# A hybrid attention and gated-MLP kernel on one core: the first four tiles are centred instead of normalised, and the value weights come in two halves

## The chip, the core and the metric

The kernel runs on one core of a Trainium2 chip. The metric is device time in microseconds (us). Three runs of the kernel before took 222.53, 222.60 and 222.67 us; the median, 222.6 us, is the time before.

The engines are named as the profile names them: PE is the matrix engine (PEld its weight loads), DVE the vector engine, ACT the scalar engine, POOL the GpSimd engine, and SP the engine that issues the DMAs (SPq in the profile).

## The reference

The input x has 2048 tokens of 512 features. It is layer-normalised without gain or bias, and two branches and the input itself are added.

```
xn  = (x - mean) / sqrt(var + 1e-5)
q, k, v = xn @ wqkv                            # 32 heads of 16 features
phi_q = [softmax(q @ w_phi), softmax(-(q @ w_phi))]      # per head
phi_k = [softmax(k @ w_phi), softmax(-(k @ w_phi))]
kv, z = sum over tokens of phi_k v, and of phi_k
A   = (phi_q kv) / (phi_q z + 1e-6) @ wo
B   = ((xn @ w_gate) * (xn @ w_up)) @ w_down   # 1792 inner features
out = x + A + B
```

## The kernel before

**Tiles.** The tokens form 16 tiles of 128. The kernel works from xnT, the normalised input with features on the partitions, four blocks of 128 features wide.

**Making xnT.** For each tile DVE takes mean and variance (L410, L412), POOL makes 1/sqrt(var + 1e-5) with a power (L419, after an addition at L417, which DVE does for tiles 0 to 3), and DVE subtracts and multiplies in one instruction (L434, `emit_xn`). Tiles 0 to 3 are then transposed by PE, four 128-column matmuls against an identity, and ACT copies the result out of PSUM (`act_op`, L277). Tiles 4 to 15 are transposed by DMA (L164), which SP issues.

**Keys and values.** `k_pe(t)` makes the values of tile t on PE (four 512-column matmuls with `wv`) and ACT copies them to `vext`. `wprime` folds the small head matrices (`wbd`, built by POOL from w_phi at L392, `make_wbd`) into the transposed key or query weights `wT`. `k_pk(t)` makes the key features on PE; `emit_exp` copies them with both signs by two ACT instructions, takes maxima on DVE (L474, L480) and exponentials on ACT; `k_norm` normalises them on DVE.

**The MLP.** `glu(g, ft)` is a unit of four token tiles (group g) by 128 inner features (ft): four 512-column matmuls for the gate, four for the up projection, an ACT copy and a DVE product (L545). `final(t)` adds the down projection and the attention output and x (DVE L642), and SP stores it.

**Queries.** `q_pk`, `q_scale`, `q_T` (a DMA transpose), `q_num` (PE, then DVE L614, L615) and `q_oT` (a DMA transpose) run tile by tile once the sums over all tokens are there.

**What sets the order.** Every operation is recorded as a step by one helper for each engine, so one line of the profile (L297 for all matmuls, L277 for all ACT work) stands for many places. `_order` then plans: each step has an estimated cost and each load a due time (`at`); whenever an engine is free in the plan, it takes the earliest ready step, and among those ready the one of lowest priority number. MLP units have numbers of 1e6 and more, so they fill holes; steps marked `urgent` (the first four tiles' normalisation and transposes) are taken up to 200 ns ahead of others. The order of each engine is then fixed, and on the chip an engine waits for its next step even when a later one could run. SP's loads all go into one hardware queue, in the order of issue.

**The start.** SP issues x of tile 0, tile 1, tiles 2 and 3, the whole `wv`, x of tiles 4 to 7, the gate and up weights of the first four units (512 KB each), w_phi, the transposed key weights `wT` (a DMA transpose), then the gate and up weights of the other ten units (1280 KB each), then the transposes of tiles 4 to 7. PE first runs 46 matmuls on zeros. Then come the transposes and values of tiles 0 to 3, four MLP units, `wprime` and four `k_pk`, and then the work on tile 4.

Of the kernel before, what the change touches and what calls it, by code (L numbers as in the profile page):

```python
# [197 lines left out]
def _build(nc, es, A_x, A_wqkv, A_w_phi, A_wo, B_w_gate, B_w_up, B_w_down, out):  # L198
# [93 lines left out]
    def mms(items, prio=None, warm=False):  # L292

        def fn(e):
            ins = None
            for o, l, r, a, z in items:
                ins = e.matmul(o, lhsT=l, rhs=r, start=a, stop=z)  # L297
            return ins
        reads = []
        writes = []  # L300
        c = 0.0
        for o, l, r, a, z in items:
            reads += [l, r]
            writes.append(o)
            c += max(25.0, o.free_size() / 2.4 + 2.3) * (1.6 if warm else 1.0)
        return sc.step(PE, fn, reads=reads, writes=writes, cost=c, lat=260.0, prio=prio)
# [40 lines left out]
    def load_gu(on, f0, n, at):  # L347
# [3 lines left out]

    load_x(SP, 0, 1, 3150.0)
    load_x(SP, 1, 1, 3700.0)
    load_x(SP, 2, 2, 4800.0)
    load_w(SP, wv_v, A_wqkv[:, 1024:1536].rearrange("(q p) j -> p q j", p=128), 6800.0)
    load_x(SP, 4, 4, 8200.0)
    load_gu(SP, 0, 4, 10800.0)
    sc.dma(SP, wphi_v, bass.AP(tensor=A_w_phi.tensor, offset=A_w_phi.offset, ap=[[16, 128], [2048, NQ], [1, 16]]),
           at=12500.0)
    load_wT(1, 14500.0)  # L360
    load_gu(SP, 4, 10, 20500.0)


    zero = sbv("tree", 0, 128)
    dve(lambda e: e.memset(zero, 0.0), [], [zero], 128)  # L365
    mms([(bank(7, 0, 128), zero, zero, True, True)] * 46, warm=True)

# [37 lines left out]
    pool(lambda e: e.memset(mhalf, -0.5), [], [mhalf], 4)  # L405

    def emit_ln_stats(t0, n):
        ts = slice(t0, t0 + n)
        for t in range(t0, t0 + n):
            dve(lambda e, t=t: e.bn_stats(stats_v[:, t, 0:6], x_tile(t)), [x_tile(t)], [stats_v[:, t, 0:6]], 512)  # L410
        for t in range(t0, t0 + n):
# [3 lines left out]
        rstd4 = rstd_v[:, ts, 0:1]  # L415
        add = dve if t0 < 4 else pool
        add(lambda e: e.tensor_scalar(out=veps.unsqueeze(2), in0=var4, scalar1=1e-5, scalar2=None, op0=ALU.add),  # L417
            [mv_v[:, ts, :]], [veps], n)
        pool(lambda e: e.tensor_tensor(out=rstd4, in0=veps.unsqueeze(2), in1=mhalf[:, 0:n].unsqueeze(2), op=ALU.pow),  # L419
# [8 lines left out]
    def next_a():  # L428
        b = a_bank[0] % a_banks[0]
        a_bank[0] += 1  # L430
        return b

    def emit_xn(t):
        dve(lambda e: e.tensor_scalar(out=xn_tile(t), in0=x_tile(t), scalar1=mv_v[:, t, 0:1],  # L434
                                      scalar2=rstd_v[:, t, 0:1], op0=ALU.subtract, op1=ALU.mult),
            [x_tile(t), mv_v[:, t, 0:1], rstd_v[:, t, 0:1]], [xn_tile(t)], 512, rate=0.5)
        if t >= 4:
            sc.dma(SP, xnT_v[:, :, t * 128:(t + 1) * 128], xn_tile(t), transpose=True, issue=1250.0, land=3200.0,
                   at=36000.0 + 1300.0 * (t - 8) if t >= 8 else 22500.0 + 1300.0 * (t - 4))
            return  # L440
        b = next_a()
        mms([(bank(b, q * 128, 128), xn_tile(t)[:, q * 128:(q + 1) * 128], ident, True, True) for q in range(NQ)])
        act_op(xnT_v[:, :, t * 128:(t + 1) * 128], bank(b).rearrange("p (q s) -> p q s", q=NQ))

# [15 lines left out]

    def emit_exp(src_bank, e_out):

# [3 lines left out]
        tr = (i % 2) * 1024  # L466
        act_op(pst[:, 0:512], bank(src_bank))
        act_op(pst[:, 512:1024], bank(src_bank), scale=-1.0)
        src = pst.rearrange("p (g k) -> p g k", g=16)
# [33 lines left out]

    def k_pe(t):
        b = next_a()
        mms(group(bank(b), [(xnT(q, t * 128, 128), wv_v[:, q, :]) for q in range(NQ)]))
        act_op(vext_all[:, t, :, 0:64], bank(b).rearrange("p (c j) -> p c j", c=8))

    def k_pk(t):
        b = next_a()  # L510
        mms(group(bank(b), [(xnT(q, t * 128, 128), Wp_v[:, 1, q, :]) for q in range(NQ)]))
        p_slot["k", t] = emit_exp(b, ek_v[:, t, :])

# [73 lines left out]
    def q_pk(t):  # L587
        b = next_q()
        mms(group(bank(b), [(xnT(q, t * 128, 128), Wp_v[:, 0, q, :]) for q in range(NQ)]))
        p_slot["q", t] = emit_exp(b, eq(t))  # L590

# [17 lines left out]
    def q_num(t):  # L609
# [4 lines left out]
        dve(lambda e: e.reciprocal(out=w, in_=nd[:, :, 64:68]), [nd[:, :, 64:68]], [w], 32, rate=6.0)  # L614
        dve(lambda e: e.tensor_tensor(  # L615
            out=o.rearrange("p (g h d) -> p g h d", g=8, h=4),
            in0=nd[:, :, 0:64].rearrange("p g (h d) -> p g h d", h=4),
            in1=w[:, :, :, None].to_broadcast([128, 8, 4, 16]), op=ALU.mult),
            [nd[:, :, 0:64], w], [o], 512)

# [7 lines left out]
    def final(t, b, cols=(0, 512)):  # L628
# [12 lines left out]
        xs = x_tile(t)[:, c0:c1]  # L641
        dve(lambda e: e.tensor_tensor(out=og, in0=ob, in1=xs, op=ALU.add), [ob, xs], [og], c1 - c0, prio=-2.0)  # L642
        sc.dma(SP, out_flat[t * 128:(t + 1) * 128, c0:c1], og, is_out=True)
# [21 lines left out]

    for t in range(4):
        first = len(sc.steps)
        ln(t, 1)
        for st in sc.steps[first:]:
            st.urgent = True  # L670
        k_pe(t)
    make_wbd()
    wprime(1)
    for b0 in range(0, NT, 4):
# [5 lines left out]
        if b0 == 0:  # L680
            load_later(lambda: load_x(SP, 8, 8, 29000.0))
        if b0 == 4:
# [187 lines left out]
```

## Time and profile before

| what | value |
|---|---|
| three runs, median | 222.6 us (222.53 to 222.67) |
| the profiled execution's own time | 222.43 us |
| its span, first to last instruction | 220.7 us |
| PE busy | 215.4 us, 1273 matmuls recorded |
| DVE busy | 192.8 us |
| ACT busy, POOL busy | 114.4 us, 9.6 us |
| DMA | 19.91 MB, 8.67 MB of it read from HBM |
| granted PE clock | 1.00 throughout |

The profile is one execution. Its page gives busy time by engine, busy shares in 40 slices of 5.5 us, the DMA queue's packets, the chain of work that ended last, and groups of instructions by line with the idle time before them. The timeline view lists instructions in order of time and merges neighbours of one kind; a line's columns are start, duration (of the merged stretch), engine, line, operation, shapes, count, and in brackets the idle time before it and what ended that. The view of DMAs gives the time from issue to landing.

### The profile page before, as it was taken

The numbers are of one execution on the slowest core, as the hardware profiler recorded it, in microseconds if no ns is written. First come the engines' busy times: TensorE is split into PE (matmuls) and PEld (weight loads), VectorE is DVE, ScalarE is ACT, GpSimd is POOL, SyncE is SP. The second block draws the span as 40 slices with busy tenths as digits, with TensorE's granted clock in tenths as the row PEclk, the third lists the DMA queues.
The fourth block names the chain that finished last, engine by engine and source line by source line (L and its number), as shares of the span: only waits on it lengthen the run. The fifth ranks groups of instructions, "written<-read, shape, count | busy, mean of one in ns | idle before, by whom it ended". The sixth has DMA issues, their size and how long they took to land.

```text
span 220.7 us, 3555 instructions
## 1 busy us (share of the span) xinstructions
PE 215.4 (98%) x1273; PEld 107.0 (48%) x1296; DVE 192.8 (87%) x552; ACT 114.4 (52%) x189; POOL 9.6 (4%) x25
## 2 busy tenths in 40 slices
PE   8899999999999999999999999999999999999995
PEld 8454444444445545444445544444445454444544
DVE  5855999999998289999999999999999999998421
ACT  2668977466442699875543676656454433230000
POOL 4250000200003000000000000000000000000000
PEclk9999999999999999999999999999999999999999
DMA  6999720139200340000000004435446556565621
GB/s 175 324 295 287 177 80 3 25 74 337 88 3 19 77 95 3 0 0 0 3 0 1 3 0 87 79 74 97 95 95 98 117 107 133 77 142 118 99 72 49
DMA packets 46386, 19.91 MB, mean 90 GB/s; under 512 B 37408, under 2 KB 45344, under 8 KB 46368
## 3 DMA queue, kind: packets, MB, share of 16 engines
q1 hardware_dynamic: 46368, 19.68, 38.5%
q8 instruction: 10, 0.16, 0.3%
q14 instruction: 8, 0.07, 0.1%
HBM read 8.67 MB, written 2.10 MB: 49 GB/s over the span
## 4 chain that ended last, share of the span: by engine, by line
PE 94%; DMA 3%; SPq 1%; issue 1%; DVE 1%
PE ps L297 94%; DMA arena<-in_A_x_dram 3%; SPq L165 1%; DVE arena L410 0%; DVE arena L434 0%; DVE arena L642 0%
## 5 line engine op out<-in xcount | busy, mean ns | idle before, releaser
L297 PE MATMUL ps<-arena 128*128 128x512 bf16 (+4 forms) x1273 | 215.4, 331 | 3.0 <-DVE arena L365 1.0
L297 PEld LDWEIGHTS ps<-arena 128*128 128x128 bf16 x1296 | 107.0, 100 | 111.2 <-ACT arena L277 2.2
L277 ACT ACTIVATE arena<-ps 128x512 bf16<-128x512 f32 (+1 forms) x156 | 83.2, 596 | 53.2 <-PE ps L297 45.3
L277 ACT ACTIVATE arena<-arena 128x1024 bf16<-128x1024 bf16 x32 | 34.3, 1082 | 28.2 <-DVE arena L480 25.9
L494 DVE TENSOR_TENSOR arena<-arena 128x512 f32<-128x512 bf16 (+3 forms) x128 | 48.8, 393 | 0.1
L545 DVE TENSOR_TENSOR arena<-ps,arena 128x512 bf16<-128x512 f32 x56 | 38.0, 679 | 3.9 <-ACT arena L277 2.2
L474 DVE TENSOR_TENSOR arena<-arena 128x512 bf16<-128x512 bf16 (+3 forms) x128 | 31.6, 269 | 4.6 <-ACT arena L277 4.4
L480 DVE TENSOR_TENSOR arena<-arena 128x1024 bf16<-128x1024 bf16 x32 | 21.5, 673 | 0.0
L642 DVE TENSOR_TENSOR arena<-ps,arena 128x512 bf16<-128x512 f32 (+2 forms) x17 | 11.1, 651 | 7.4 <-PE ps L297 7.2
L410 DVE BATCH_NORM_STATS2 arena<-arena 128x6 f32<-128x512 bf16 x16 | 10.7, 681 | 1.5 <-DMA arena<-in_A_x_dram 1.5
L521 DVE TENSOR_TENSOR arena<-arena 128x1024 bf16<-128x1024 bf16 x16 | 10.9, 680 | 0.0
L615 DVE TENSOR_TENSOR arena<-ps,arena 128x512 bf16<-128x512 f32 x16 | 10.8, 673 | 0.1
L614 DVE RECIPROCAL arena<-ps 128x32 f32<-128x32 f32 x16 | 5.6, 348 | 3.7 <-PE ps L297 3.5
L518 DVE RECIPROCAL arena<-arena 128x64 bf16<-128x64 f32 x16 | 8.6, 539 | 0.0
L434 DVE TENSOR_SCALAR arena<-arena 128x512 bf16<-128x512 bf16 x16 | 6.1, 406 | 2.2 <-issue 1.5
L601 DVE TENSOR_TENSOR arena<-arena 128x512 bf16<-128x512 bf16 x16 | 6.5, 407 | 0.0
L419 POOL TENSOR_TENSOR arena<-arena 128x1 f32<-128x1 f32 (+1 forms) x7 | 5.3, 764 | 4.1 <-DVE arena L417 3.8
L598 DVE RECIPROCAL arena<-arena 128x32 f32<-128x32 f32 x16 | 5.4, 336 | 0.0
L417 POOL TENSOR_SCALAR arena<-arena 128x4 f32<-128x4 f32 x3 | 1.1, 380 | 55.1 <-DVE arena L412 55.1
L599 DVE TENSOR_TENSOR arena<-arena 128x32 bf16<-128x32 f32 x16 | 2.7, 171 | 0.0
L412 DVE BATCH_NORM_AGGREGATE arena<-arena 128x2 f32<-128x6 f32 x16 | 2.0, 160 | 0.1
L561 DVE TENSOR_TENSOR arena<-ps,arena 128x65 f32<-128x65 f32 x8 | 1.6, 220 | 0.4 <-PE ps L297 0.4
(19 smaller groups left out, 9.8 us busy)
## 6 DMA issues: line engine op xcount, KB each, us to landing
out_dram<-arena SPq DMA_DIRECT2D x15, 128.0 KB, 2.0
arena<-in_B_w_down_dram SPq DMA_DIRECT2D x1, 1792.0 KB, 7.5
arena<-in_B_w_gate_dram SPq DMA_DIRECT2D x1, 1280.0 KB, 6.8
arena<-in_B_w_up_dram SPq DMA_DIRECT2D x1, 1280.0 KB, 10.3
arena<-in_A_x_dram SPq DMA_DIRECT2D x1, 1024.0 KB, 5.4
arena<-arena SPq DMA_TRANSPOSE x44, 2.8
arena<-in_A_wqkv_dram SPq DMA_DIRECT2D x1, 512.0 KB, 4.2
arena<-in_A_x_dram SPq DMA_DIRECT2D x1, 512.0 KB, 5.7
```

The source lines that it names most:

```text
L277: return e.activation(out=out_ap, in_=in_ap, func=func, scale=scale, **kw)
L297: ins = e.matmul(o, lhsT=l, rhs=r, start=a, stop=z)
L410: dve(lambda e, t=t: e.bn_stats(stats_v[:, t, 0:6], x_tile(t)), [x_tile(t)], [stats_v[:, t, 0:6]], 512)
L474: dve(lambda e, dst=dst, src=src, k=k: e.tensor_tensor(out=dst, in0=src[:, :, 0:k], in1=src[:, :, k:2 * k], op=ALU.max), [src], [dst], 16 ...
L480: dve(lambda e: e.tensor_tensor(out=p4, in0=p4, in1=src[:, :, None, :].to_broadcast([128, 16, 16, 4]), op=ALU.subtract), [pst, src], [pst] ...
L494: dve(lambda e, dst=dst, src=src, k=k: e.tensor_tensor(out=dst, in0=src[:, :, 0:k], in1=src[:, :, k:2 * k], op=ALU.add), [src[:, :, 0:2 * ...
L518: dve(lambda e: e.reciprocal(out=rs, in_=sm), [sm], [rs], 64, rate=6.0)
L521: dve(lambda e: e.tensor_tensor(out=e4, in0=e4, in1=r4[:, :, None, :].to_broadcast([128, 16, 16, 4]), op=ALU.mult), [ek_v[:, t, :], rs], [ ...
L545: dve(lambda e: e.tensor_tensor(out=dst, in0=bank(bu), in1=gr, op=ALU.mult), [bank(bu), gr], [dst], 512, prio=-1.0)
L601: dve(lambda e: e.tensor_tensor(out=e1, in0=e1, in1=rs[:, :, None, :].to_broadcast([128, 8, 16, 4]), op=ALU.mult), [e1, rs], [e1], 512, ra ...
L615: dve(lambda e: e.tensor_tensor(out=o.rearrange("p (g h d) -> p g h d", g=8, h=4), in0=nd[:, :, 0:64].rearrange("p g (h d) -> p g h d", h= ...
L642: dve(lambda e: e.tensor_tensor(out=og, in0=ob, in1=xs, op=ALU.add), [ob, xs], [og], c1 - c0, prio=-2.0)
```

## The change

- **Centring.** Tiles 0 to 3 are centred only (`x - mean`, `emit_centred`). The factor 1/sqrt(var + 1e-5), called rstd, is still made (`emit_root`, both steps on POOL) and is put back later: as the scale of ACT's copies of the values and of the key and query features, while the MLP's product of two unscaled projections is multiplied by rstd squared in `final`, together with the attention output, which `q_num` has divided by rstd squared beforehand. One DVE reciprocal of four numbers (`emit_squares`) gives rstd squared.
- **Sign copy.** For these tiles the second copy in `emit_exp`, with the minus sign, reads the first copy in SBUF instead of PSUM.
- **Tile 1's mean** comes from ACT, as a copy of x with scale 1/512 into PSUM bank 6 and a running sum; its variance is taken by DVE after the centring.
- **Tile 0's transposes** go in two halves of two feature blocks, each with a copy of its own. Its first matmuls with `wv` are split in two steps likewise.
- **Values of tiles 0 and 1** are made in two halves of 256 columns, the second halves after the transposes of tile 2.
- **Loads.** `wv` comes in two halves of 256 columns, x of tiles 2 and 3 in a load each between them; the first gate and up weights go ahead of x of tiles 4 to 7. The due times are changed.
- **Warm-up.** 28 matmuls on zeros instead of 46, and three more after tile 0's transposes; in the plan such a matmul costs 1.92 instead of 1.6 times a fast one.

```diff
-    load_x(SP, 0, 1, 3150.0)
-    load_x(SP, 1, 1, 3700.0)
-    load_x(SP, 2, 2, 4800.0)
-    load_w(SP, wv_v, A_wqkv[:, 1024:1536]..., 6800.0)
-    load_x(SP, 4, 4, 8200.0)
-    load_gu(SP, 0, 4, 10800.0)
+    load_x(SP, 0, 1, 3000.0)
+    load_x(SP, 1, 1, 3450.0)
+    load_wv(0, 4800.0)
+    load_x(SP, 2, 1, 5200.0)
+    load_x(SP, 3, 1, 5600.0)
+    load_wv(1, 6800.0)
+    load_gu(SP, 0, 4, 9600.0)
+    load_x(SP, 4, 4, 11000.0)
     sc.dma(SP, wphi_v, ...,
-           at=12500.0)
-    load_wT(1, 14500.0)
-    load_gu(SP, 4, 10, 20500.0)
+           at=11200.0)
+    load_wT(1, 13100.0)
+    load_gu(SP, 4, 10, 19500.0)
...
-    mms([(bank(7, 0, 128), zero, zero, True, True)] * 46, warm=True)
+    mms([(bank(7, 0, 128), zero, zero, True, True)] * 28, warm=True)
...
+    def emit_centred(t):
+        mean = mv_v[:, t, 0:1]
+        if t == 1:
+            mean = lnt_v[:, 2, 8:9]
+            sc.step(ACT, lambda e: e.activation(out=bank(6), in_=x_tile(t), func=ACTF.Copy, scale=1.0 / 512.0,
+                                                accum_out=mean), ...)
+        else:
+            emit_moments(t)
+        dve(lambda e: e.tensor_scalar(out=xn_tile(t), in0=x_tile(t), scalar1=mean, scalar2=None, op0=ALU.subtract), ...)
...
+    def emit_root(t):
+        pool(lambda e: e.tensor_scalar(out=veps(t), in0=mv_v[:, t, 1:2], scalar1=1e-5, scalar2=None, op0=ALU.add), ...)
+        pool(lambda e: e.tensor_tensor(out=rstd_v[:, t, 0:1], in0=veps(t), in1=mhalf[:, 0:1], op=ALU.pow), ...)
...
+    def scale_of(t):
+        return rstd_v[:, t, 0:1] if t < RAW else 1.0
...
-                   at=36000.0 + 1300.0 * (t - 8) if t >= 8 else 22500.0 + 1300.0 * (t - 4))
+                   at=36000.0 + 1300.0 * (t - 8) if t >= 8 else 21500.0 + 600.0 * (t - 4))
...
-        act_op(pst[:, 0:512], bank(src_bank))
-        act_op(pst[:, 512:1024], bank(src_bank), scale=-1.0)
+        act_op(pst[:, 0:512], bank(src_bank), scale=scale_of(t))
+        act_op(pst[:, 512:1024], bank(src_bank) if t >= RAW else pst[:, 0:512], scale=-1.0)
...
+        if t < RAW:      # q_num
+            dve(lambda e: e.scalar_tensor_tensor(out=o4, in0=n4, scalar=veps(t), in1=w4, op0=ALU.mult, op1=ALU.mult), ...)
+            return
...
+        if t < RAW:      # final
+            r2 = lnt_v[:, 2, t:t + 1]
+            dve(lambda e: e.scalar_tensor_tensor(out=og, in0=ob, scalar=r2, in1=xs, op0=ALU.mult, op1=ALU.add), ...)
...
-    for t in range(4):
+    for t in range(RAW):
         first = len(sc.steps)
-        ln(t, 1)
+        emit_centred(t)
+        emit_T(t, 2 if t == 0 else 1)
         for st in sc.steps[first:]:
             st.urgent = True
-        k_pe(t)
+        if t == 0:
+            mms([(bank(7, 0, 128), zero, zero, True, True)] * 3, warm=True).deps.append(sc.by_eng[PE][-2])
+        if t == 1:
+            emit_moments(t)
+        emit_root(t)
+        if t < 2:
+            k_pe(t, 5 + t, 0, 256)
+        else:
+            if t == 2:
+                for s in (0, 1):
+                    k_pe(s, 7 if s == 0 else next_a(), 256, 512)
+            k_pe(t)
     make_wbd()
+    emit_squares()
     wprime(1)
```

## The prediction

> **What bounds the kernel now.** I read the page's busy times first, then the chain, then the timeline of the first 23 us, then the DMA view.
>
> ```profile
> PE 215.4 (98%) x1273; PEld 107.0 (48%) x1296; DVE 192.8 (87%) x552; ACT 114.4 (52%) x189; POOL 9.6 (4%) x25
> PE 94%; DMA 3%; SPq 1%; issue 1%; DVE 1%
> ```
>
> PE is the bound. In the chain in order of time PE starts late and then hardly stops:
>
> ```profile
> 2.70 5.72 DMA arena<-in_A_x_dram
> 8.44 0.69 DVE arena L410
> 9.14 0.33 DVE arena L434
> 9.51 6.47 PE ps L297 x44
> ```
>
> From 9.51 us on the chain is PE to the end but for gaps of 0.05 us. So a change of the start is worth what it takes from the time PE is not doing useful work before that point, if PE can be fed afterwards. The timeline shows what PE does before:
>
> ```profile
> 1.04 5.79 PE L297 MATMUL ps<-arena 128*128 128x128 bf16 x54 [1.04 <-DVE arena L365]
> 3.65 0.18 DVE L412 BATCH_NORM_AGGREGATE arena<-arena 128x2 f32<-128x6 f32 x1
> 4.10 0.56 POOL L419 TENSOR_TENSOR arena<-arena 128x1 f32<-128x1 f32 x1 [1.95 <-DVE arena L417]
> 4.75 0.38 DVE L434 TENSOR_SCALAR arena<-arena 128x512 bf16<-128x512 bf16 x1
> 6.59 1.09 ACT L277 ACTIVATE arena<-ps 128x512 bf16<-128x512 f32 x2 [4.53 <-PE ps L297]
> 7.47 22.75 PE L297 MATMUL ps<-arena 128*128 128x512 bf16 x119 [0.64 <-ACT arena L277]
> ```
>
> Tile 0 is normalised at 5.13, but the 46 zero matmuls run until 6.0 (the single matmuls start 0.107 us apart), and the first value matmul starts at 7.47. In single matmuls, 512 columns take 0.216 us start to start and 128 columns 0.056 us from 6.4 us on. The first MLP gate starts at 11.47. Then come four units (32 x 0.216 = 6.91), `wprime` (16 x 0.056 = 0.89) and four `k_pk` (16 x 0.216 = 3.45): 11.25, which ends at 22.72. There stands the second limit:
>
> ```profile
> 22.70 7.24 PEld L297 LDWEIGHTS ps<-arena 128*128 128x128 bf16 x35 [0.31 <-DMA arena<-arena]
> arena<-arena SPq DMA_TRANSPOSE x1, 9.2
> arena<-in_B_w_up_dram SPq DMA_DIRECT2D x1, 1280.0 KB, 10.3
> ```
>
> The second line is tile 4's transpose, issued at 13.51 and landed 9.2 us later, at 22.66; the third the second up load, issued at 11.89, landed at 22.17. Both move in one queue that is busy from 1.9 to 23.5 us. PE reaches tile 4 (22.72) just as it lands. An earlier PE therefore runs into this landing.
>
> **The head, part by part.** Landings are those of the DMAs in the trace. Tile 0's x is there at 2.90. L410 and L412 end at 3.83; centring follows at once (0.035 between dependent DVE instructions) and ends at 4.25 instead of 5.13: POOL's part, 0.9, is off the path. 28 zero matmuls end at 1.04 + 28 x 0.107 = 4.03. Transposes of tile 0: 4.31 to 4.74 at 0.107 each. The half copies are unseen; 128x65 takes 0.22 on ACT and 128x512 0.6, so 256 columns 0.39. The first ends at 5.15, the second at 5.42.
>
> Tile 1's mean on ACT is unseen: from 0.54 (half of the 128x1024 copy with exponential, 1.08) to 1.3 (all of it and one more small instruction of 0.22); I take 0.8, by the 128x512 copy of 0.6 and the small one. x lands at 3.30, so 4.15, and DVE is busy to 4.25 anyway; centred at 4.65, transposed 4.74 to 5.17. At 1.3 it is 0.4 later, inside the wait below. Three zero matmuls follow to 5.49, then tile 0's first value half (two steps of 2 x 0.213, cold), to 6.36; tile 1's half needs its copy (6.0) and runs to 6.8.
>
> DVE goes on: tile 1's statistics to 5.36, tile 2's L410, L412, L434 (0.69, 0.18, 0.38 and gaps) to 6.69, tile 3's to 7.96; before, tile 3 was centred at 9.45, because L410 of tile 4 stood ahead of it and waited for its x (8.42). Tile 2 is transposed at 6.8 to 7.02, the second value halves run to 7.9 (8 x 0.108), tile 3's transposes to 8.25, values of tile 2 to 9.1, of tile 3, after their copy, from 9.16 to 10.0. Halves cost no PE time: 8 x 0.108 for 4 x 0.216; if a 0.10 us weight load showed each time, 0.8 at most, half of it in the wait below.
>
> Loads for this: before, 1 MB of x and `wv` landed by 6.37. Two more issues of some 0.47 each stand on SP, so `wT` is issued at 6.1 instead of 5.11, still ahead of the queue. 512-byte packets are unseen: 256 bytes take 18 ns and 1024 bytes 50, so 29, and 1024 packets in place of 512 cost 0.26 spread over 16 engines; from nothing to 1.6 if each took 50. First `wv` half at 4.8, second at 6.7: in time. The first gate and up weights come ahead of tiles 4 to 7 (512 KB, 1.45): up at 10.0, needed at 10.9.
>
> **The first gate at 10.03 instead of 11.47: 1.44 us.** The same 11.25 ends at 21.28. `wphi` and `wT` landed at 11.61 and 13.39; `wprime` comes at 13.5, and POOL is free for `wbd` since tile 4's root comes later.
>
> **What is late next.** Tiles 4 to 7 land at 11.5 instead of 8.42. Four L410 (0.6 each) between MLP products, POOL's 1.4 and L434 give tile 4 at 17.2 instead of 13.48, and SP issues its transpose then. The queue works on the second gate and up loads until about 20 us, so I expect no loss, and a landing at 22.66 plus 0.2 for packets: 22.86. Before it PE has one piece. I walked the plan by hand with the costs and due times in the code, for the order alone: in it PE is free at 21.25, the second gate weights are due at 19.5 and tile 4 at 21.5, so gate 4 goes first, 0.86, to 22.15 (its weights landed at 18.03). Its up half does not: at 22.1 in the plan tile 4 is ready and ranks first. PE then waits 0.7 and starts tile 4 at 22.92. Before, it started at 22.72 with 0.863 less done. **Gain: 0.863 - 0.20 = 0.66 us.** The wait hides up to 0.7 of error in my head.
>
> **The rest.** ACT's copies with a scale and eight sign copies from SBUF (0.54 to 0.62 for 0.6, 0.2 longer where the second waits for the first): ACT is busy 13.0 of 14 us between 16 and 30, but the bank is free one copy earlier; nothing. Eight DVE products with PSUM (L615, L642, 0.67) take a further scalar: the small scalar form takes 0.216 and a plain product of 128x64 0.219, so nothing; at double time 5.4, against 19 us at the end in which DVE works 8.16. They read the same elements, so no gain. One reciprocal, under 0.35; four additions of 0.15 leave DVE. The middle of the kernel must follow:
>
> ```profile
> 66.00:77.00 11.00, 10.89 (x106) 6.04 (x106) 6.43 (x18) 4.80 (x14) 1.72 (x2) 1.00 0.24 48
> 77.00:150.00 73.00, 72.58 (x420) 34.89 (x426) 71.16 (x212) 49.04 (x82) 0.00 (x0) 1.00 0.13 27
> 200.00:219.00 19.00, 18.39 (x116) 9.52 (x115) 8.16 (x19) 0.00 (x0) 0.00 (x0) 1.00 0.46 89
> ```
>
> These are busy times by stage (length, PE, PEld, DVE, ACT, POOL). DVE is nearly full from 77 on, but idles 4.6 us between 66 and 77 because PE feeds it; so it starts its dense stretch earlier by what PE gains. The end stays: last product at 218.48, then the store.
>
> **Sum.** The profiled execution took 222.43 (span 220.7 and 1.7 around it), 0.17 under the median; 222.43 - 0.66 = 221.77, by the median 221.9. Measurement can tell about 0.2%, 0.45 us, from no change.
>
> **The clock.** Matmuls of 128 columns are 0.107 us apart until 6.4 and 0.056 after: full speed came 5.4 us after the first. The Trainium skill, "TensorE: Matmul & The Clock Gate", Part 1: The HAM clock gate, says that the array runs at half clock until a free-running window of about 3.4 us has been busy. The trace agrees so far as it goes: 5.4 lies between one such window and two. The rule speaks against fewer zero matmuls with a hole at 4.03 to 4.31; by it full speed could come one window later, at 6.4 + 3.4 = 9.8, an estimate, and the sum would be no gain, 222.6.
>
> **Rivals.**
> 1. *The clock stays cold, or the plan puts tile 4 ahead of gate 4: no change.* If the hole restarts the 5.4 us, full speed comes at 9.7, and 3.45 us of work after 6.36 takes 1.5 longer (3.34 us of it at half speed); gate 4 ends at 23.6, against 22.72 + 0.86 = 23.58 before. Without gate 4 in the hole PE simply waits for 22.86. Both give 222.6 to 222.8. For it: the hole, and only 0.25 us between the plan's 21.25 and 21.5. Against it: PE is busy over 90% of 1.04 to 6.4.
> 2. *Transposes land early.* Around 20 to 22 us the queue moves 39 to 118 GB/s in its slices, with tile 4's packets mixed into the end of the up load. If a transpose issued at 17.2 spares that, it lands before 22.15, and all 1.44 stay: 221.2. Against it: the queue still holds both by 18.5.
> 3. *Slower: the queue ends later.* SP's `wT` issue takes 6.1 us before. If that is SP's own time, the second loads go out 0.95 later; with 0.26 for packets tile 4 lands at 23.9. From 23.53 on, the landing costs one for one: +0.35, 222.9; with 50 ns packets 224.3. For it: SP issues right after it, at 11.28. Against it: the other `wT` took 1.9 us on an idle queue, so the first seems held by the queue.
>
> **Chances.** Forecast 0.43 (own range 221.4 to 222.4; most of it, 0.37, over the bound); rival 2 0.20; rival 1 0.20; rival 3 0.17. So faster 0.57, same 0.26, slower 0.17. The range reaches from rival 2 to rival 3's nearer end: 221.1 to 223.0.
>
> **What would show it.** First gate at 10.0; gate 4 at 21.3; a wait of PE on the DMA transpose near 22.1 to 22.9; tile 4's transpose issued at 17; `wT` issue ending near 11.4 (rival 3: 12.2); 0.056 us spacing by 6.5. The forecast is wrong if PE waits elsewhere after 23 us, for steps the plan reordered.

## The result and the profile after

The changed kernel takes **224.14 us** (median of 9 runs, 223.02 to 224.79) against 222.62 (9 runs, 222.50 to 223.03): the ratio on record is 1.0052, with a 95% interval of 1.0030 to 1.0074 (the two medians alone give 1.0068). It is slower by about half a per cent; the forecast was 221.9. The profiled execution took 223.88 us (span 222.1; before 222.43 and 220.7).

The page of the changed kernel, busy times and chain by engine, then pieces of the chain in order of time (start, length, what):

```profile
PE 214.9 (97%) x1266; PEld 105.7 (48%) x1289; DVE 193.0 (87%) x549; ACT 116.6 (52%) x194; POOL 10.7 (5%) x29
PE 82%; DMA 7%; DVE 5%; issue 2%; SPq 2%; POOL 1%; ACT 0%; DVEq 0%
4.78 7.88 DMA arena<-in_A_x_dram
23.20 3.48 DMA arena<-arena
187.64 4.99 DMA arena<-arena
192.68 5.65 PE ps L297 x39
```

PE is no longer the whole chain from 9.51 us on. The chain now runs through the load of x of tiles 4 to 7, then through DVE's normalisation of them to tile 7's transpose, and breaks a third time at 187.64, in a transpose that PE reaches at 192.68. The timeline of the changed kernel:

```profile
3.46 0.60 ACT L424 ACTIVATE ps<-arena 128x512 f32<-128x512 bf16 x1 [1.39 <-DMA arena<-in_A_x_dram]
3.99 0.19 ACT L424 ACTIVATION_READ_ACCUMULATOR ps<-arena 128x1 f32 x1
5.33 1.59 SPq L165 DMA_DIRECT2D arena<-in_A_w_phi_dram  x1
6.96 5.49 SPq L164 DMA_TRANSPOSE arena<-in_A_wqkv_dram  x1
7.67 6.45 PE L297 MATMUL ps<-arena 128*128 128x256 bf16 x35 [0.70 <-DMA arena<-in_A_wqkv_dram]
14.91 11.61 PE L297 MATMUL ps<-arena 128*128 128x128 bf16 x63 [0.78 <-POOL arena L398]
18.62 5.84 SPq L164 DMA_TRANSPOSE arena<-arena  x4
23.75 2.27 PEld L297 LDWEIGHTS ps<-arena 128*128 128x128 bf16 x12 [0.51 <-DMA arena<-arena]
26.73 1.47 PE L297 MATMUL ps<-arena 128*128 128x512 bf16 x6 [0.21 <-DMA arena<-arena]
192.68 1.51 PE L297 MATMUL ps<-arena 128*128 128x68 bf16 x13 [0.79 <-DMA arena<-arena]
```

The first two rows are tile 1's mean: 0.72 us from the start of the one to the end of the other (0.8 was expected). Tile 0's transposes start at 4.33, the first value matmul at 5.31. Then come PE's waits, told by single matmuls: 0.87 for the second half of `wv` (landed 7.63; expected 6.7), 0.95 for `wbd`, which POOL builds as soon as `wphi` has landed (12.87; before 11.61), 0.19 for tile 4's transpose (landed 23.71; before 22.66), 0.38 for tile 7's, and 0.95 at 192.68 for the transpose of tile 11's query features. The first gate starts at 10.51, 0.96 earlier than before, and gate 4 runs ahead of tile 4, as the hand-walked plan had it. PE is ready for tile 4 only at 23.57: most of its delay there comes from the waits for `wv` and `wbd`, the last 0.19 from the transpose's own landing.

**The sum from the landings.** Tile 4 starts at 23.76 with gate 4 (0.863) already done; before, it started at 22.72 without it: 23.757 - 0.863 - 22.722 = +0.17. With the later waits of 0.38 and 0.95 that is +1.50; the last matmul moved by 219.64 - 218.22 = +1.42. Nothing else moved the time by more than 0.1.

### The profile page after: what moved, and what is told of

Read it like the earlier page. It is cut to its first block, busy times and chain, and to the rows that moved or that the text cites. A ratio compares the mean times of both kernels' runs of the same rounds, so it can differ in the third digit from the quotient of the medians.

```text
span 222.1 us, 3563 instructions
## 1 busy us (share of the span) xinstructions
PE 214.9 (97%) x1266; PEld 105.7 (48%) x1289; DVE 193.0 (87%) x549; ACT 116.6 (52%) x194; POOL 10.7 (5%) x29
## 4 chain that ended last, share of the span: by engine, by line
PE 82%; DMA 7%; DVE 5%; issue 2%; SPq 2%; POOL 1%; ACT 0%; DVEq 0%
PE ps L297 82%; DMA arena<-arena 4%; DMA arena<-in_A_x_dram 4%; SPq L165 2%; DVE arena L521 1%; DVE arena L451 1%; DVE arena L595 1%; POOL arena L459 0%; DVE arena L483 0%; DVE arena L700 0%; DVE arena L541 0%; DVE arena L527 0%; ACT arena L277 0%; DVE arena L672 0%; DVE arena L651 0%
## 5 line engine op out<-in xcount | busy, mean ns | idle before, releaser
L297 PE MATMUL ps<-arena 128*128 128x512 bf16 (+5 forms) x1266 | 214.9, 330 | 5.0 <-DVE arena L371 1.0
L277 ACT ACTIVATE arena<-ps 128x512 bf16<-128x512 f32 (+2 forms) x137 | 72.4, 588 | 49.2 <-PE ps L297 38.7
L277 ACT ACTIVATE arena<-arena 128x1024 bf16<-128x1024 bf16 (+1 forms) x40 | 38.7, 979 | 27.9 <-DVE arena L527 27.6
L595 DVE TENSOR_TENSOR arena<-ps,arena 128x512 bf16<-128x512 f32 x56 | 38.1, 680 | 2.7 <-PE ps L297 2.4
L521 DVE TENSOR_TENSOR arena<-arena 128x64 bf16<-128x64 bf16 (+3 forms) x128 | 31.8, 273 | 3.1 <-ACT arena L277 2.8
L700 DVE TENSOR_TENSOR arena<-ps,arena 128x512 bf16<-128x512 f32 (+2 forms) x13 | 8.4, 644 | 7.3 <-PE ps L297 7.2
L277 ACT ACTIVATE arena<-ps,arena 128x512 bf16<-128x512 f32 (+1 forms) x14 | 8.2, 623 | 4.5 <-PE ps L297 4.5
L672 DVE TENSOR_TENSOR arena<-ps,arena 128x512 bf16<-128x512 f32 x12 | 8.2, 685 | 0.1
L483 DVE TENSOR_SCALAR arena<-arena 128x512 bf16<-128x512 bf16 x12 | 4.4, 410 | 2.3 <-POOL arena L459 2.3
L459 POOL TENSOR_TENSOR arena<-arena 128x4 f32<-128x4 f32 x3 | 3.1, 1042 | 0.3
L697 DVE SCALAR_TENSOR_TENSOR arena<-ps,arena 128x512 bf16<-128x512 f32 x4 | 3.0, 746 | 0.0
## 6 DMA issues: line engine op xcount, KB each, us to landing
arena<-in_B_w_up_dram SPq DMA_DIRECT2D x1, 1280.0 KB, 10.1
```

The costliest lines, as they stand in the source:

```text
L277: return e.activation(out=out_ap, in_=in_ap, func=func, scale=scale, **kw)
L521: dve(lambda e, dst=dst, src=src, k=k: e.tensor_tensor(out=dst, in0=src[:, :, 0:k], in1=src[:, :, k:2 * k], op=ALU.max), [src], [dst], 16 ...
L595: dve(lambda e: e.tensor_tensor(out=dst, in0=bank(bu), in1=gr, op=ALU.mult), [bank(bu), gr], [dst], 512, prio=-1.0)
L672: dve(lambda e: e.tensor_tensor(out=o4, in0=n4, in1=w4, op=ALU.mult), [nd[:, :, 0:64], w], [o], 512)
```

## The experiments

Every number of a wait is from single matmuls of that run's profile; the ratios are to the kernel before on the same chip, in runs shared by all kernels of one batch. Three theories stood at first. **Q**: the smaller and more numerous first loads leave the DMA queue short of work at the start, and all that follows in it lands a microsecond late. **X**: it is the place of x of tiles 4 to 7 behind the gate and up weights. **C**: it is the changed compute and its re-planned order, of which the wait at 192 is the sign. The loads ahead of `wphi` are written below in the order of issue; a slash separates loads, g and u are the first gate and up weights, 4-7 is x of tiles 4 to 7, wv0 and wv1 the halves.

| run | loads | KB moved by 8 us | wT's issue ends | tile 4 lands | ratio (95%) |
|---|---|---|---|---|---|
| before | 0/1/2-3/wv/4-7/g/u | 1842 | 11.22 | 22.66 | 1 |
| after | 0/1/wv0/2/3/wv1/g/u/4-7 | 1672 | 12.45 | 23.71 | 1.0052 (1.0030 to 1.0074) |
| e1 | the same | 1634 | 12.29 | 23.76 | 1.0031 (1.0006 to 1.0056) |
| e2 | as before | 1823 | 11.32 | 22.50 | 1.0004 (0.9984 to 1.0025) |
| e3 | 0/1/wv0/2/3/wv1/4-7/g/u | 1522 | 12.71 | 24.23 | 1.0063 (1.0039 to 1.0087) |
| e4 | e3's, old compute | 1367 | 13.70 | 24.99 | 1.0113 (1.0071 to 1.0156) |
| e5 | as before | 1800 | 11.22 | 22.80 | 0.9984 (0.9964 to 1.0003) |
| e6 | as after | 1518 | 13.06 | 24.97 | 1.0033 (1.0017 to 1.0048) |
| e7 | as before | 1839 | 11.35 | 22.83 | 0.9972 (0.9958 to 0.9985) |
| e8 | 0/1/wv/2-3/4-7/g/u | 1759 | 11.25 | 22.77 | 0.9990 (0.9977 to 1.0003) |
| e9 | 0/1/2/3/g/u/4-7; ACT wv0/wv1 | 1929 | 10.86 | 22.41 | 1.0017 (0.9999 to 1.0035) |
| e10 | 0/1/wv/2/3/g/u/4-7 | 1714 | 12.49 | 24.14 | 1.0048 (1.0030 to 1.0065) |
| e11 | 0/1/wv0/2-3/wv1/g/u/4-7 | 1546 | 12.41 | 23.73 | 1.0047 (1.0031 to 1.0064) |
| e12 | 0/1/2-3/wv/g/u/4-7 | 1862 | 11.38 | 22.70 | 1.0010 (0.9982 to 1.0039) |
| e13 | 0/1/2/3/wv/4-7/g/u | 1743 | 11.60 | 23.39 | 1.0113 (1.0066 to 1.0160) |
| e14 | 0/wv0/2/g/u/4-7; ACT 1/3/wv1 | 1898 | 11.18 | 22.74 | 0.9965 (0.9942 to 0.9988) |
| e15 | as e9 | 1960 | 10.76 | 22.37 | 0.9976 (0.9953 to 0.9999) |
| e16 | as e9, ACT later | 1760 | 11.59 | 22.97 | 1.0045 (1.0020 to 1.0071) |
| e17 | as e14 | 1903 | 11.34 | 22.84 | 0.9957 (0.9942 to 0.9971) |

### e1 to e4: which part loses the time

e1 is the changed kernel as it is.

> The changed kernel once more, for a second profile and for times beside the runs below. Theory Q (the DMA queue): the two extra and smaller loads at the start leave the queue short of work between 4.5 and 6 us, all that is behind them lands about 1 us later, tile 4's transpose at 23.7 instead of 22.66, and that eats the gain of the head. Theory X: the damage is x of tiles 4 to 7 standing behind the gate and up weights, so that its transposes are issued 5 us later. Theory C: the compute part costs (scaled copies, products with a third operand, the order that the planner makes of them), and the queue is hidden. All three expect 223.0 to 224.8 here. The wait of 0.95 us at 192 us on query tile 11's transpose: Q and X take it for chance (an instruction fetch of 1.4 us on one DMA engine beside it) and expect it in some profiles, C expects it in every one.

e2 takes back the loads only:

```diff
-    load_wv(0, 4800.0)
-    load_x(SP, 2, 1, 5200.0)
-    load_x(SP, 3, 1, 5600.0)
-    load_wv(1, 6800.0)
-    load_gu(SP, 0, 4, 9600.0)
-    load_x(SP, 4, 4, 11000.0)
+    load_x(SP, 2, 2, 5200.0)
+    load_w(SP, wv_v, A_wqkv[:, 1024:1536]..., 4800.0)
+    load_x(SP, 4, 4, 11000.0)
+    load_gu(SP, 0, 4, 9600.0)
```

> The changed kernel with the loads of before in their order: x of tiles 0, 1, 2 and 3 together, the value weights whole, x of tiles 4 to 7, then gate and up. The due times in the plan stay, so the order of the engines stays but for the second halves of tile 0's and 1's values, which come ahead of tile 2's transposes. Theory Q: tile 4's transpose lands at 22.7 again and tile 7's at 24.1, gate 4 stands before it, so 222.6 - 0.8 = 221.8 (221.4 to 222.2). Theory X: the same, 221.8. Theory C: 223.5 or more, since the compute part is all there.

e3 moves `load_x(SP, 4, 4, 11000.0)` ahead of `load_gu(SP, 0, 4, 9600.0)`, no more.

> The changed kernel with one exchange: x of tiles 4 to 7 goes ahead of the first gate and up weights again; the small loads stay, and the order of every other engine is the same. Theory Q: the queue is as late as in the changed kernel, tile 4's transpose lands at 23.5 to 23.8; only the wait of 0.4 us for tile 7's goes: 223.3 to 223.9. Theory X: tile 4's x lands near 9.3, its transposes are issued 4 us earlier, and the time falls below that of before, 221.8 to 222.3. Theory C: no change from the changed kernel.

e4 is the kernel before with `wv` in two halves between x of tiles 1, 2 and 3, as in e3.

> The kernel before with one thing of the change: the value weights in two halves of columns between the x tiles, x of tiles 2 and 3 in a load each; x of tiles 4 to 7 still ahead of gate and up. Due times and the order of the engines are those of before. Theory Q: everything behind the small loads lands about 1 us later, tile 4's transpose at 23.6; PE has nothing to put before it, so 222.6 + 0.9 = 223.5 (223.2 to 223.8). Theory X and theory C: 222.6, within 0.3.

e1 repeated the waits (1.16 for the second half of `wv`, 0.49 for `wbd`, 0.42 for tile 4, 0.55 near 192). **X fell**: e3 has x of tiles 4 to 7 where it was and is as slow as the changed kernel. **Q held in e4**: the new loads alone, under the old compute, make it 1.1% slower. Part of that is the granted clock, which fell in three of e4's six runs; the three with clock 1.00 took 224.15 to 224.50 against 222.90, 0.6 to 0.7%. e2 put every landing up to tile 4's transpose back to where it was, and PE waited for no tile; yet it came out equal to before, not 1 us faster. So either C held, or something else ate the gain. The profiles of e2 and e5 suggest which.

### e5 and e7: the slow array behind e2's hole

In e2 PE has nothing to do from 5.42 to 6.46, until `wv` lands whole at 6.32. e5 puts 14 zero matmuls in place of 3 there:

```diff
-            mms([(bank(7, 0, 128), zero, zero, True, True)] * 3, warm=True)...
+            mms([(bank(7, 0, 128), zero, zero, True, True)] * 14, warm=True)...
```

> The changed compute with the loads of before, as in e2, and 14 zero matmuls instead of 3 after tile 0's transposes, so that PE is not empty while it waits for wv. Theory K (e2's gain was eaten by the half clock: its 128-column matmuls stayed at 0.107 us until 10.04, with PE empty from 5.42 to 6.46): full speed before 7, first gate near 10.2 instead of 10.4 with all of the cold work behind it, last PE instruction 0.3 to 1.5 us before e2's 219.21, time 222.0 to 222.5. Rival P (the loss of the new version lies in the reordered plan and its longer instructions after 23 us, not in the head): as e2, 223.1. Both: PE still waits 0.4 to 0.95 near 192 for the transpose of tile 11's query features.

e7 is e5 with e6's number of the plan (below).

> e5 and e6 together: the changed compute, the loads of before, 14 zero matmuls, the later place of tile 11's sums. If Q, K and C all hold: first gate near 10.2, gate 4 ahead of tile 4 without a wait, no wait near 192; 221.3 to 221.9, under the kernel before (222.9 on the chip used so far). If P holds: 222.6 or more.

PE's groups by shape between 6.4 and 10.1 us, first e2, then e5 (count, busy us, mean ns):

```profile
L297 PE MATMUL ps<-arena 128*128 128x256 bf16 x16 | 3.7, 408 | 0.8 <-DMA arena<-in_A_wqkv_dram 0.8
```

```profile
L297 PE MATMUL ps<-arena 128*128 128x256 bf16 x16 | 2.2, 272 | 0.0
```

The same 16 matmuls of 256 columns take 3.7 us in e2 and 2.2 in e5. In single matmuls of e2 they start 0.213 apart until 10.04, and at 0.109, full speed, only after that; the granted clock in the record is 1.00 all the while, so this half speed is seen in the spacing alone. The first gate starts at 12.13 in e2 and at 10.80 in e5. It is the mechanism of the prediction's rival 1, near its time (9.7 was worked out there), but behind a hole of 1.04 us instead of 0.3. The Trainium skill, "TensorE: Matmul & The Clock Gate", Part 1: The HAM clock gate, has a free-running window of about 3.4 us decide; the runs agree so far: full speed came at 3.78 (e1) and 5.14 us (after) in two executions of one kernel, at 6.4 in before, and at 10.2 and 10.4 in e2 and e15, which have holes of 1.0 and 0.9.

The hole alone does not decide. e7's profile has one of 1.04 and e8's one of 1.24, but there full speed had come ahead of the hole (4.9 and 4.7), and it stayed. By these profiles, whether an execution loses the time depends on whether full speed comes ahead of the hole, and when it comes differs between executions of one kernel. e2's runs, but for one of 226.27, lie between 222.06 and 223.74, and its profile is of one that took 223.43.

e5 is 0.2% and e7 0.3% below e2's ratio; the intervals of e2 and e5 overlap, and e7's lies wholly under 1. So the changed compute is not slower when the loads are left as they were and the hole is filled: C, as the main cause, fell. That it pays by itself is not shown, because in e5 and e7 gate 4 no longer stands ahead of tile 4 in the plan. PE waits 0.78 and 0.88 for tile 4's transpose (landed 22.80 and 22.83), here in e7:

```profile
6.83 15.33 PE L297 MATMUL ps<-arena 128*128 128x256 bf16 x96 [0.87 <-DMA arena<-in_A_wqkv_dram]
22.88 9.45 PE L297 MATMUL ps<-arena 128*128 128x512 bf16 x43 [0.71 <-DMA arena<-arena]
```

Tile 4 starts with the same work done as before, at 22.84 (e5) and 22.88 (e7) for 22.72, and the last matmuls of these profiles (218.23 and 218.27) are where before's is (218.22). They do not show where e7's 0.3% comes from.

### e6 and e15: the wait at 192

One number of the plan, so that q_num(11) stands seven matmuls later:

```diff
-        sc.dma(SP, eT(t), eq(t), transpose=True, issue=1250.0, land=3300.0)
+        sc.dma(SP, eT(t), eq(t), transpose=True, issue=1250.0, land=4600.0 if t == 11 else 3300.0)
```

> The changed kernel with one number of the plan altered: the transpose of tile 11's query features is taken to land 4600 ns after its issue instead of 3300, which puts seven matmuls (1.5 us) between tile 11's sums and where they stood. Theory C (the wait near 192 is on the path, 0.95 and 0.55 in two profiles of this version): no wait there, time 0.5 to 0.95 less, 222.8 to 223.2 where the changed kernel took 223.65. Rival: what is saved there is waited for at the next DVE-fed step, since DVE is over 95% busy in that stage: time unchanged, 223.65. Theory Q (queue short of work at the start): the head's waits for wv (0.9 to 1.2) and tile 4 (0.2 to 0.4) are unchanged.

> e9 (wv issued by ACT) with tile 11's sums placed later as in e6. Theory C (the 0.93 us that e9's PE waited near 191 is on the path): 0.5 to 0.9 less than e9: a ratio of 0.998 to 0.9995 to the kernel before, where e9 had 1.0017. Rival (that wait falls in some executions only): as e9.

In both the wait is gone. e6's time did not move (1.0033 beside 1.0031 and 1.0052). In its profile tile 4 landed 1.2 later than in e1 and PE waited 0.85 for it, but that is one run of twelve, so e6 does not show that the wait costs time. e15 against e9, the same edit, went from 1.0017 to 0.9976, 0.9 us, as long as the wait in e9 (0.93), but in another batch. So the wait is on the path in the profiles that have it (after's sum comes out only with it), while what its removal saves, and how often it falls, is not settled; e5, with the old place of tile 11's sums, does not show it. In after, e1, e2, e3, e9, e10, e12 and e13, which show it, an instruction-fetch packet of 16 KB (0.96 to 1.38 us on one DMA engine) was under way between 187.4 and 192.3, while tile 11's transpose was in flight; in e5 it came at 186.6. But e11 shows the wait (0.87) with that packet at 187.0, so the packet is not shown to be the cause.

### e8 to e13: what starves the queue

Busy times by stage (length, PE, PEld, DVE, ACT, POOL, granted clock, DMA share, GB/s), of before, then of the changed kernel:

```profile
4.00:5.00 1.00, 1.00 (x12) 1.00 (x11) 0.96 (x4) 0.00 (x0) 0.56 (x1) 1.00 0.96 285
5.00:6.00 1.00, 1.00 (x12) 1.00 (x11) 0.96 (x5) 0.00 (x0) 0.56 (x1) 1.00 1.06 363
```

```profile
4.00:5.00 1.00, 0.88 (x9) 0.65 (x8) 0.98 (x4) 0.41 (x3) 0.92 (x2) 1.00 0.89 238
5.00:6.00 1.00, 0.92 (x12) 0.57 (x9) 0.96 (x3) 0.99 (x4) 0.08 (x1) 1.00 0.76 203
```

In the changed kernel the 16 DMA engines are idle a quarter of the time from 5 to 6 us (share 0.76), with nine loads issued by 5.28. Their packets are no slower: one of 512 bytes took 27 ns, one of 1024 bytes 46 to 50. So the engines stood between packets. e9 keeps every DMA and lets ACT issue two of them:

```diff
-        load_w(SP, wv_v[:, :, c], A_wqkv...
+        load_w(ACT, wv_v[:, :, c], A_wqkv...
```

> The changed kernel with its two halves of wv issued by ACT (free until x of tile 1 lands) instead of SP: the same DMAs with the same packets, but two engines issue them; the order on PE, DVE and POOL is the changed kernel's. Theory Q1 (the queue runs empty between 4 and 6 us because SP alone issues small loads, one per 0.45 to 0.5 us): 320 GB/s or more from 5 to 6 us (changed kernel 203 and 224 in two profiles), second wv half landed by 6.7, the wT issue ended by 11.8, tile 4's transpose landed 22.7 to 23.0; time 0.7 to 1.0 under the changed kernel's 223.65: 222.7 to 222.95. Theory Q2 (the half-column loads with their 512-byte packets move slowly, whoever issues them): rate and landings as in the changed kernel, tile 4 at 23.7, 223.6.

e10 (whole `wv`, x of tiles 2 and 3 apart) and e11 (`wv` in halves, x of tiles 2 and 3 together) change SP's first megabyte from six loads to five:

> The changed kernel with wv whole (1-KB packets) between x of tile 1 and x of tile 2: five issues by SP for the first megabyte instead of six. Q1 (issues): halfway, 5 to 6 us at 260 to 300 GB/s, tile 4 near 23.2, 223.1 to 223.4. Q2 (packets): as with the loads of before, over 320 GB/s, tile 4 at 22.5 to 22.8; 222.5 to 222.9.

> The changed kernel with x of tiles 2 and 3 in one load between the two halves of wv (512-byte packets for wv): five issues. Q1 (issues): as e10, tile 4 near 23.2, 223.1 to 223.4. Q2 (packets): as the changed kernel, 203 to 224 GB/s from 5 to 6 us, tile 4 at 23.7, 223.6.

e9's stages, then e10's:

```profile
3.00:4.00 1.00, 1.00 (x12) 0.94 (x9) 0.72 (x2) 0.12 (x1) 0.00 (x0) 1.00 1.13 354
4.00:5.00 1.00, 0.60 (x6) 0.33 (x4) 0.51 (x2) 0.50 (x1) 0.67 (x2) 1.00 1.16 324
```

```profile
5.00:6.00 1.00, 0.57 (x7) 0.40 (x6) 0.28 (x1) 0.94 (x3) 0.04 (x1) 1.00 1.05 350
6.00:7.00 1.00, 1.00 (x10) 0.90 (x11) 0.75 (x2) 0.37 (x1) 0.00 (x0) 1.00 0.95 280
```

With two issuers the queue is full from 3 us, `wv` is whole at 5.38, wT's issue ends at 10.86 and tile 4 lands at 22.41: 1.3 earlier than in the changed kernel, with the same packets. So **it is not the packets (Q2), and a second issuer takes the loss away**. Tile 4 is reached without a wait, behind gate 4, at 22.90:

```profile
7.61 20.63 PE L297 MATMUL ps<-arena 128*128 128x128 bf16 x116 [0.17 <-DVE arena L429]
```

Why the second issuer helps is not shown. That SP alone issues too slowly (Q1) does not fit SP's own rows: by 5.0 us it had finished the issue of 2048 KB, of which 792 KB had moved, while the first load's packets began 0.6 us after its issue ended. The loads of ACT may also be served beside those of SP; no run separates the two.

The time moved less than the landing, to 1.0017: x of tile 1 now landed at 4.47, beside ACT's loads, PE waited 0.60 and 0.74 for tiles 0 and 1, and 0.93 near 192. Two notes of the Trainium skill bear on this. "Perfetto Trace Analysis", DMA Optimizations, says that balancing DMAs over the engines that can issue them may help where the making of descriptors is the limit: e9's landings came earlier, though no run shows what the limit was. "DMA: Bandwidth & Descriptors", Rules for kernel authors, says that spreading DMAs over engines does not help bandwidth and only saves issue time: here 1929 KB had moved by 8 us for 1672, and tile 4 landed 1.3 us earlier.

But e10 and e11, expected halfway, were as slow as the changed kernel. Is it the count of loads, or the gate weights ahead of x of tiles 4 to 7, which both share? e12 keeps four loads and the gate ahead, e13 five loads and x of tiles 4 to 7 ahead:

> The changed kernel with the first megabyte in the four loads of before (x of tile 0, of tile 1, of tiles 2 and 3, whole wv), but the gate and up weights still ahead of x of tiles 4 to 7. Theory N (the number of loads that SP puts into the one queue at the start is what drives the 16 DMA engines apart; four do no harm, five or six do, of whatever packets): first to last landing of the gate load within 1 us, tile 4's transpose near 22.5, PE without a wait for it, 222.7 to 223.1 as e2. Theory O (the place of the gate and up loads does it): the gate load's landings 2 us apart, tile 4 at 23.7 or later, 223.7.

> The changed kernel with x of tiles 2 and 3 in a load each, whole wv behind them, then x of tiles 4 to 7 ahead of gate and up: the loads of before but for one more. Theory N: tile 4's transpose at 23.5 to 24.2, 223.5 to 223.9. Theory O: tile 4 near 22.5, 222.7 to 223.1.

e12's landings are those of before: O fell. e13's queue is nearly that of before too (11.60), so up to `wT` five loads alone do no harm when the small ones all come first: N, as a rule of count, fell as well. The pair e10 and e13 speaks against Q1 too: by 2.5 us SP had issued 768 KB in e10 and 384 in e13, from 3.2 us on as much, and yet wT's issue ended 0.9 later in e10. e13's tile 4 landed 0.55 behind the second up load (22.84), as before (0.49); why that load was late is not shown. The four small loads put `wv` at 7.17, PE stood for 2.33 us, and then this happened (e13, columns as above, the granted clock third from the end):

```profile
6.00:7.00 1.00, 0.00 (x0) 0.00 (x0) 0.95 (x2) 0.00 (x0) 0.83 (x2) 1.00 0.97 332
8.00:9.00 1.00, 1.00 (x7) 0.74 (x5) 0.45 (x2) 0.73 (x2) 0.92 (x3) 0.50 1.09 369
10.00:11.00 1.00, 1.00 (x8) 0.82 (x7) 0.00 (x0) 0.56 (x1) 0.00 (x0) 0.50 1.84 256
```

The granted clock itself fell to 0.50. The mean granted clock of the whole run is 0.991 to 0.992 in all four runs of e13, in three of e4's six (0.985 to 0.992) and in six of e16's twelve, the versions with the longest holes at the start; so e4's and e13's 1.1% is not the queue's alone. One run each of e5, e6 and the kernel before and two of e12 show 0.992 as well.

What all versions share is in the table: where 1714 KB or less has moved by 8 us, wT's issue ends at 12.3 or later, and where 1743 or more, by 11.6; and tile 4's landing follows that end by 11.2 to 11.9 us in every run. The two groups are close in these KB, but they differ in how far the 16 engines drift apart: the engines' landings of the gate load lie 1.6 to 2.8 us apart in the late group (2.1 in after), and 0.7 to 1.3 in the other (1.1 in before) but for e16 (1.6). The transpose of `wT` pays for the drift. Its packets start near 10 us in before and after alike, but they come at full rate (about 290 GB/s) only when the last engine is through with the loads: from 11.5 us in before and from 12.5 in the changed kernel, where the queue moved 98 GB/s from 11 to 12 us. Why small loads behind or between the halves of `wv` drive the engines apart, and small loads ahead of it do not, stays open.

e8 moves whole `wv` ahead of x of tiles 2 and 3, in four loads, and keeps e6's number of the plan:

> As e7, but instead of the extra zero matmuls (3 as in the changed kernel) the whole wv is issued ahead of x of tiles 2 and 3: four issues for the first megabyte, 1-KB packets. Theory Q: the queue is not short, wv lands near 5.6, x of tiles 2 and 3 near 6.4, up weights near 11.4, tile 4's transpose near 22.5; PE has work from 5.6 on, tile 2 centred near 7.5; first gate 10.0 to 10.3; 221.3 to 221.9. If the wait that is left (5.4 to 5.6, and for tile 2) holds the clock down as in e2: full speed at 10, 222.8 to 223.2.

The up weights (11.44) came as said and tile 4 (22.77) nearly so, but `wv` landed at 6.13 for 5.6 and x of tiles 2 and 3 at 6.88 for 6.4: PE waited 1.24, then 0.69 and 0.54 for tiles 2 and 3. Full speed was there at 4.7, so neither of the two expectations came out: 0.9990.

### e14, e16 and e17: does the change pay with two issuers?

e14 shares the first six loads between SP and ACT and keeps e6's number of the plan; e17 adds zero matmuls (10 for 3) to it; e16 is e15 with ACT's two loads held back until its table load is over, and 5 zero matmuls for 3. e14's edit:

```diff
-        load_w(SP, wv_v[:, :, c], A_wqkv[...
+        load_w(ACT if half else SP, wv_v[:, :, c], A_wqkv[...
...
-    load_x(SP, 1, 1, 3450.0)
+    load_x(ACT, 1, 1, 3450.0)
...
-    load_x(SP, 3, 1, 5600.0)
+    load_x(ACT, 3, 1, 5600.0)
```

> The changed kernel with its loads in the same pieces, issued by two engines: SP x of tile 0, first wv half, x of tile 2, then as before; ACT x of tile 1, of tile 3, second wv half; and tile 11's sums placed later as in e6. Theory N: three loads for each issuer, so the queues stay full, wv's second half before 5.5, tile 4's transpose near 22.4, no wait near 192; x of tile 1 earlier than in e9 (4.47), so less of PE's waits of 0.66 and 0.80 there; 221.8 to 222.3. Rival (what PE gains in the head it waits for at tile 4, which lands no earlier than 22.4): 222.3 to 222.6.

> e15 with ACT's two wv issues placed behind its table load (a one-column copy ahead of them), so that x of tiles 0 and 1 have the queues to themselves, and 5 zero matmuls instead of 3. Theory Q1 (what counts is that a second engine issues): tile 1's x back at 3.4, so the wait for its centring (0.99 in e15 at 5.78) goes; wv's halves near 5.0 and 5.6; full speed by 6.6; tile 4's transpose near 22.4, PE without a wait there; 221.3 to 221.8, a ratio of 0.994 to 0.996. If the clock starts late all the same (as in e15's profile, half speed until 10.8): as e15, 222.2.

> e14 with 10 zero matmuls instead of 3 after tile 0's transposes, to fill PE's hole of 0.98 us before tile 1. If the half clock after that hole is what spreads e14's times (221.3 to 223.2): the spread shrinks and the median falls to 221.6 to 222.0. Rival: the extra matmuls delay tile 1 by what they save, 222.2 as e14.

e16 missed: ACT's second load was issued behind SP's gate weights in time (2.75 against 2.66) and landed at 9.03, PE waited 1.70, and the clock fell in half of its runs. e14 gave 222.22 and **e17 221.84 us against 222.55**, a ratio of 0.9957 (0.9942 to 0.9971): faster than both kernels. The chain of e17 by engine, and PE from 4.2 us on:

```profile
PE 97%; DMA 1%; DVE 1%; issue 0%
```

```profile
4.89 23.33 PE L297 MATMUL ps<-arena 128*128 128x128 bf16 x137 [0.69 <-DVE arena L429]
```

After 4.89 PE waits for nothing by more than 0.1 us, neither for `wv`, for tile 4 (landed 22.84) nor near 192. This profile shows that the waits are gone, not where the gain lies: it is of e17's slowest run (222.68; the six took 221.33 to 222.68), in which full speed came only at 9.1 and tile 4 started at 23.96 behind gate 4, which is 0.38 later than before once gate 4's 0.863 is taken off. The kernel before was not run with two issuers, so how much of the 0.43% is the changed compute is not known.

## Why the prediction was wrong

- **The head was nearly right.** Tile 0 centred, tile 1's mean, the hole: as said. Full speed by 6.5 (5.14) was luck, with 3.8 to 10.4 in the runs above. The first gate came at 10.51 for 10.03; the wait of 0.87 for `wv` is more than that.
- **The plan was right, and so was the sum where the queue is mended.** Gate 4 stands ahead of tile 4. In e9's profile PE starts tile 4 at 22.90 (22.92 was forecast) with gate 4 done: 0.69 gained there, for 0.66. That it is so close is partly luck, since PE came 0.75 later than forecast and the transpose landed 0.45 earlier. The gain then goes in the 0.93 near 192.
- **The step that failed** is "The queue works on the second gate and up loads until about 20 us, so I expect no loss, and a landing at 22.66 plus 0.2 for packets: 22.86". It landed at 23.71. The prediction had counted two more issues of 0.47 on SP and put them "still ahead of the queue". SP's issues did stay ahead, but that did not keep the engines at work, as the prediction took it to do: they stood for part of 4.5 to 6 us, 170 KB were missing at 8 us, `wv` came 0.9 later than said, `wphi` 1.26 later than the old landing that was taken over, x of tiles 4 to 7 1.2 later (12.66 for 11.5), wT's issue ended at 12.45 for 11.4. The forecast's gain of 0.66 became a loss of 0.17 there. e2 (old loads, old landings), e4 (new loads alone, slower) and e9 (a second issuer, every landing from the gate weights to tile 4's transpose 1.3 us or more earlier) show that it is these loads from one issuer; why the engines stand stays open.
- **Rival 3 had the place, and by luck the size, of tile 4's landing** (23.9; its 222.9 in all is too low) but not the mechanism: wT's issue is not SP's own 6.1 us. It took 5.49, 7.17 (e10) and 6.07 us (e9), and ended 0.35 to 0.52 before `wphi`'s last landing each time: the queue holds it.
- **Two waits had no term**: 0.38 for tile 7, whose transpose was issued at 23.20 behind the late x, and 0.95 near 192. The prediction named "if PE waits elsewhere after 23 us, for steps the plan reordered" as what would break it. With tile 4's 0.85 they make 2.18; the forecast for the profiled execution (221.77) was 2.11 under its 223.88.
- **Rival 1's clock** did not decide here, but by its profile did in e2. Its other half, tile 4 ahead of gate 4, is what e5 and e7 had.
- **Rival 2** read 39 to 118 GB/s "around 20 to 22 us"; the view of before has 310 from 20.0 to 20.5 and these figures from 20.5 on. Tile 4's transpose landed before 22.15 in no run.
- The terms put at nothing were small: the final product with a scalar (L697) took 746 ns and that of `q_num` (L669) 699, where plain products were put at 670; the reciprocal took 0.18, under the bound of 0.35.

## What to carry to other kernels

Do not take a queue to be full because its issuer is ahead of it: look at the DMA share of the first stages. Here cutting and rearranging the first loads cost more than a microsecond at the far end, because every later transfer follows in the same queue. Where the first loads must be small, try letting a second engine issue some of them, and keep the matrix engine busy until they land. Before a step that is moved is called free, look for what the queue carries behind it and who waits for the last of that.

## What the runs showed of the hardware

- A hole of 1.04 us in PE's work early on, ahead of full speed (e2), left the array at half speed for 3.6 us more with a granted clock of 1.00 in the record; holes of 1.04 (e7) and 1.24 (e8) behind the start of full speed left it as it was; a hole of 2.33 us (e13), also behind it, brought the granted clock itself to 0.50 for some 4 us.
- A single SP issued a load in 0.40 to 0.51 us in the changed kernel, whether it was of 128 or 512 KB. By these, 128-KB loads alone would feed 128 KB / 0.47 us = 0.28 MB per us (an estimate), under the 0.36 that the queue moved when full; the changed kernel's first six loads, 1 MB in 2.84 us, were fed at 0.37.
- A DMA transpose behind loads reaches full rate when the last of the 16 engines has finished what stands before it: in the changed kernel the queue moved 98 GB/s from 11 to 12 us and 289 from 12.5 on.
- ACT's running sum is read by a second instruction of 0.19 us.
